# Sparse attention and a Sinkhorn mixture of experts on one core: four edits of order

## The chip, the core and the metric

The kernel runs on one core of a Trainium2 chip. A core has five engines with queues of their own: TensorE (PE in the profile, with its weight loads as PEld), VectorE (DVE), ScalarE (ACT), GpSimd (POOL) and SyncE (SP). They run side by side and wait for each other through semaphores. Matmuls write into PSUM banks; all other tiles lie in SBUF. The metric is the time of one execution on the device, in microseconds (us).

## What is computed

First eight heads of attention over four batches of 576 tokens. Four heads see the 32 tokens up to and with their own; the other four see every 32nd token up to their own. The result, 2304 tokens of 512 values, is x. Then a gate over eight experts, made even over tokens and experts in eight rounds, and the experts.

```python
scores = np.where(masks[None, :, :, :], scale * q @ k.T, -1000000000.0)
attn = np.exp(scores - np.max(scores, axis=-1, keepdims=True))
attn = attn / (np.sum(attn, axis=-1, keepdims=True) + 1e-09)
x = (attn @ v).transpose(0, 2, 1, 3).reshape(2304, 512)

logits = x @ w_gate
P = np.exp(logits - logits.max())
for _ in range(8):
    P /= P.sum(1, keepdims=True) + 1e-09
    P /= P.sum(0, keepdims=True) + 1e-09
    P *= N / E
for e in range(8):
    out += P[:, e:e + 1] * (np.maximum(x @ w1[e], 0.0) @ w2[e])
```

## The kernel before, in words

**Two parts for precision.** Every operand of a large matmul is held as a high part (ScalarE copies it to the matmul's own type) and a low part (source minus high part, made by VectorE or POOL). A product is then three matmuls: high by high, high by low, low by high.

**The start and the slots.** Attention runs in 32 units (batch, pair of heads, half), one after the other. For each: a load of queries and keys (qk) and one of values (v) by load_qkv, the scores on PE, the mask and the smallest value on VectorE (L247, which reads the constants cst), the exponential on ScalarE (L259), the normalization on POOL (L270), transposes on PE (L282, against the identity in cst), the product with the values (L295, L309), and x in two parts (L331 on ScalarE, L336 on VectorE). The first eight units stand in a loop of their own (at_k to WARM). Behind it come 36 slots. A slot takes 256 tokens and one of four column blocks of the first half of expert 0: its first layer (L417), the second layer of the slot before (L454), and, while there are units left, a unit's values, the next unit's scores, and then the transposes and the normalization of units between. The table `work` adds further pieces to the end of a slot.

**Units of x sums.** The rest of the experts runs with Strassen's scheme: 768 tokens at a time (a pass; there are three) and 256 columns (a pair of 128), seven products instead of eight. The sums of x that it needs are made by build_s for 128 tokens at a time, as one of the pieces in `work`: in one slot two L532 and four L548 on POOL, in the next slot a high part on ScalarE (L551) and a low part on VectorE (L553), and in the one after that two stores (L556). Units for passes 0 and 1 stand in slots named in a list.

**Steps.** After the slots, step(g) runs for each group g, 30 groups in each pass. A step finishes the first layer of the group before (finish_first), begins its own seven products (ba, bb and bc are their banks; L698) and does the second layer of the group before. In pass 0 the second layer is an ordinary one (second, L730), and the step also prepares the weights of the next group: load_w1g brings the raw W1 (ra, rb), prep_w1 makes three sums on POOL (L616, L619, L620) and splits all four (L177 on ScalarE, L178 on POOL); load_w2g brings the raw W2, whose sums (L649 to L653) and low parts VectorE makes. In passes 1 and 2 the prepared weights come back from memory, and the second layer is Strassen's too (second_strassen, L849): its seven left sides are a11, a22, a12 and the four sums s1 to s4, each with a high part (L830, ScalarE) and a low part (L834, POOL). In finish_first the sums themselves are made on POOL (L906 to L910) out of the gated results u3, m1, r11 and u2. Their order on POOL is the order of the program. The first group of a pass copies its second products with ScalarE (total, L855) in place of adding them with VectorE (L857).

**The gate's rounds.** The generator `gat` gives one round of the eight at each next(gat): a small product (L382) between VectorE's reductions and divisions (L374 to L386). The last rounds run in step 0.

**Queues.** SP issues all loads and stores in the order of the program, except the first constants, which ScalarE's queue issues (L1061). A DMA that must wait holds up those behind it on its queue. The sets of PSUM banks are named t, l1, s and y, two banks each.

Of the kernel before, what the change touches and what calls it, by code (L numbers as in the profile page):

```python
# [55 lines left out]
def kernel(  # L56
# [9 lines left out]
    nc = tc.nc  # L66
    P = 128
    NT, D = out.shape
    E, _, F = w1.shape
# [32 lines left out]
    cst = const.tile([P, 4, P], F32, name="cst")  # L102
# [54 lines left out]
    def load_w2(t, e, f0):  # L157
        nc.sync.dma_start(t, w2[e, f0 : f0 + P, :])
# [37 lines left out]
    qkv_t, sms, sums_t, pts, moved, mxs = {}, {}, {}, {}, {}, {}  # L196

    def load_qkv(k):
        if k < NS:
            nq, nk, nv = _columns(*steps[k][1:])  # L200
            t = pools["qkv"].tile([P, QK], F32, tag="qk", name=f"qk_{k}", bufs=3)
            nc.sync.dma_start(t[:, : nq + nk], qkv[k, :, : nq + nk])
            tv = pools["qkv"].tile([P, 5 * 2 * DH], F32, tag="v", name=f"v_{k}", bufs=5)
            nc.sync.dma_start(tv[:, :nv], qkv[k, :, nq + nk : nq + nk + nv])
            qkv_t[k] = t, tv[:, :nv].rearrange("p (w j d) -> p w j d", j=2, d=DH)
# [270 lines left out]
    at = W1N  # L476
# [29 lines left out]
    for p in range(NPASS):  # L506
        for k in range(NK):
            k = (k - KEEP * p) % NK
# [61 lines left out]
    def load_w1g(g):  # L570
        if g >= NK or g in wraw:
            return
        _, e, j, _ = groups[g]
        if g < 2:
            t = raw_slots(4).rearrange("p (n i k f) -> p n i k f", n=4, i=2, k=2)
            wraw[g] = [t[:, i] for i in range(4)]
        else:
            wraw[g] = [
                pools["hg" if g == 2 else "rab"].tile(
                    [P, 2, 2, P], F32, tag=f"r{x}", name=f"r{x}_{g}",  # L580
                    bufs=2 if g > 2 and x in "ab" else 1,
                )
                for x in "abtu"
            ]
        ra, rb = wraw[g][:2]
        for t, i, dh, fh in ((ra, 0, 0, 0), (ra, 1, 1, 1), (rb, 0, 0, 1), (rb, 1, 1, 0)):
            f0 = f_at(g, fh)
            nc.sync.dma_start(
                t[:, i],
                w1[e, 2 * P * dh : 2 * P * (dh + 1), f0 : f0 + P].rearrange("(k p) f -> p k f", p=P),  # L590
            )

    def load_w2g(g):
        if g >= NK:
            return
        _, e, j, _ = groups[g]
        o = 2 * D * ((g + 1) % 2)
        w2raw[g] = raws[:, o : o + 2 * D]
        for i in range(2):
            load_w2(w2raw[g][:, i * D : (i + 1) * D], e, f_at(g, i))  # L600
# [109 lines left out]
    def turning(g):  # L710

        return g >= NK and g % NK == NK - LAST[groups[g][0]]
# [119 lines left out]
    def form_lo(g, name, src):  # L832
        t = hg[g, name]
        nc.gpsimd.tensor_tensor(t[:, 1], src, t[:, 0].bitcast(F32), op=ALU.subtract)  # L834
# [49 lines left out]
    def finish_first(g, s):  # L884

        m1, u2, u3, bb, bc = part.pop(g)
        mul(g, "t4", "x22", bb, False)
        if s:
            gated(g, u3, u3, 1)
            form_hi(g, "a22", u3)  # L890
        plus(m1, bb, m1)
        if s:
            gated(g, m1, m1, 1)
        else:
            relu_hi(g, 1, 0, m1)
        mul(g, "w22", "s4", bc, False)
        plus(u2, bc, u2)
        if not s:
            relu_hi(g, 0, 1, u2)
            return ((1, 0, m1), (0, 1, u2))  # L900
        gated(g, u2, u2, 0)
        r11 = r11s.pop(g)
        s1, s4 = (
            pools["late"].tile([P, TN], F32, tag=x, name=f"{x}_{g}") for x in ("s1t", "s4t")
        )
        nc.gpsimd.tensor_tensor(s1, m1, u3, op=ALU.add)  # L906
        nc.gpsimd.tensor_tensor(m1, m1, r11, op=ALU.subtract)
        nc.gpsimd.tensor_tensor(r11, s1, r11, op=ALU.subtract)
        form_lo(g, "a22", u3)
        nc.gpsimd.tensor_tensor(s4, u2, r11, op=ALU.subtract)  # L910
        return ("a12", u2), ("s2", r11), ("s3", m1), ("s1", s1), ("s4", s4)

    def step(g):
# [2 lines left out]
        s = strassen(G)  # L916
        w1n, w2n = prep_w1(g + 1), prep_w2(g)
        if new:
            load_w1g(g + 2)
            if G in spans:  # L920
                load_gate(spans.index(G) + 1)
        late = ()
# [2 lines left out]
        if g >= NK:  # L925
            next(w1n, None)
        load_w2g(g + 1)
        if turning(G):
            combine()
        if new:  # L930
            m1, u2, u3 = (
                pools["u"].tile([P, TN], F32, tag=x, name=f"{x}_{g}", bufs=2)
                for x in ("m1", "u2", "u3")
            )
# [123 lines left out]
        load_qkv(at_k + 2)  # L1058

    WARM = 2 * NP - 1  # L1060
    nc.scalar.dma_start(cst[:, :2], consts[:, :2])  # L1061
    load_qkv(0)
    load_qkv(1)
    load_w()
    load_qkv(2)
    load_w()
# [61 lines left out]
    def at(i, f, *x):  # L1128
        work.setdefault(i, []).append(lambda: f(*x))

    gat = gating()
    units = [(p, k, P * th) for p in range(2) for k in range(2) for th in range(3)]
    for x, i in zip(units, (8, 9, 10, 11, 12, 13, 18, 19, 20, 21, 22, 23)):
        w = build_s(*x, P, True)
        for n in range(3):
            at(i + n, next, w, None)
# [7 lines left out]
    ):  # L1144
        at(i, load_x, 0, name)
    at(29, lambda: later_store.pop()())
    at(34, load_w1g, 2)
    at(28, load_w2g, 0)
    for i in (27, 27, 28, 28, *range(29, 35)):
        work.setdefault(i, []).insert(0, lambda: next(gat))  # L1150
# [76 lines left out]
    for g in range(NG + 1):  # L1227
# [20 lines left out]
        if 0 < p < NPASS:  # L1248
            i = n - 3
# [85 lines left out]
```

## Time and profile before

| | |
|---|---|
| three runs shown | 1550.41, 3234.23, 3856.46 us (median 3234.23) |
| the profiled execution | 1549.56 us |
| its span, first to last instruction | 1547.4 us, 25973 instructions |
| mean granted clock of TensorE | 1.00 of full speed |
| PE busy | 1535.4 us (99%) |
| weight loads (PEld) busy | 1456.0 us (94%) |
| VectorE busy | 1312.3 us (85%) |
| POOL busy | 1054.9 us (68%) |
| ScalarE busy | 548.1 us (35%) |
| moved by DMA | 430.49 MB, mean 278 GB/s |
| chain that ended last | PE 97%; POOL, DVE, DMA and issue 1% each |

How to read it: every share is of the span. The chain is the work that ended last, followed back from the last instruction; at each step it goes to what released it. Matmuls are pipelined, and their ends are modelled, so a wait of PE can also show as a group of matmuls that takes longer than the same group elsewhere. An idle time in front of an instruction stands in brackets, with what ended it.

### The profile page before, as it was taken

The page shows a single profiled execution, that of the slowest core. Times are in us where ns is not written, and L with a number is a line of the kernel's source. Part 1 is how long each engine was busy: PE and PEld are TensorE (multiplying, and loading weights), DVE is VectorE, ACT ScalarE, POOL GpSimd, SP SyncE. Part 2 cuts the span into 40 slices and gives each one's busy share as a digit, 9 for nine tenths or more (in the row PEclk, how much of TensorE's full clock was granted, in tenths as well). Part 3 has the DMA queues.
Part 4 walks back from the last instruction along what each step waited for, and adds up shares of the span by engine and source line. Part 5 has one row for each costly group of instructions (what it writes and reads, how often), then busy time and mean ns, then how long its engine had stood idle before and what let it go on. Part 6 is the DMA issues. An engine that isn't in the chain of part 4 may idle for free.

```text
span 1547.4 us, 25973 instructions
## 1 busy us (share of the span) xinstructions
PE 1535.4 (99%) x9188; PEld 1456.0 (94%) x9188; DVE 1312.3 (85%) x2552; ACT 548.1 (35%) x1299; POOL 1054.9 (68%) x1069
## 2 busy tenths in 40 slices
PE   7999999999999999999999999999999999999999
PEld 6888889898989898999999999999999999999998
DVE  5676699999999999868888888888688888888888
ACT  6666244343434343333232223223322332222221
POOL 4387255555656556168888888887777777877874
PEclk9999999999999999999999999999999999999999
DMA  7577977988989898887877777776676766766662
GB/s 226 179 235 237 377 285 289 350 324 314 327 318 328 318 328 324 299 318 274 305 282 289 267 279 286 266 283 255 245 277 262 294 256 243 284 245 246 280 241 93
DMA packets 144704, 430.49 MB, mean 278 GB/s; under 512 B 34912, under 2 KB 89280, under 8 KB 129600
## 3 DMA queue, kind: packets, MB, share of 16 engines
q1 hardware_dynamic: 144432, 428.71, 74.4%
q8 instruction: 73, 1.20, 0.3%
q14 instruction: 55, 0.45, 0.1%
q10 hardware_dynamic: 144, 0.13, 0.0%
HBM read 284.05 MB, written 144.75 MB: 277 GB/s over the span
## 4 chain that ended last, share of the span: by engine, by line
PE 97%; POOL 1%; DVE 1%; DMA 1%; issue 1%; ACT 0%; SPq 0%; POOLq 0%; DVEq 0%
PE p L849 27%; PE bb L698 18%; PE yg L730 17%; PE bc L698 12%; PE ba L698 12%; PE y L454 3%; PE ph L417 3%; PE tp L282 1%; DMA qk<-in_qkv 1%; PE sc L234 1%; PE pv L295 1%; PE pl L345 1%; PE pv L309 1%; PE sc L220 1%; POOL sm L270 0%
## 5 line engine op out<-in xcount | busy, mean ns | idle before, releaser
L857 DVE TENSOR_TENSOR total<-p,total 128x384 f32<-128x384 f32 x770 | 400.7, 557 | 0.8 <-PE p L849 0.8
L698 PE MATMUL bb<-reg 128*128 128x384 f32 x1620 | 325.8, 335 | 0.0
L698 PEld LDWEIGHTS bb<-reg 128*128 128x128 f32 x1620 | 285.0, 188 | 2.8 <-DVE u L772 0.3
L698 PE MATMUL bc<-reg 128*128 128x384 f32 x1080 | 216.4, 334 | 0.0
L698 PE MATMUL ba<-reg 128*128 128x384 f32 x1080 | 216.2, 334 | 0.0
L830 ACT ACTIVATE a<-u 128x384 fp32r<-128x384 f32 x114 | 59.9, 526 | 384.1 <-DVE u L824 382.6
L772 DVE TENSOR_TENSOR u<-bb,m 128x384 f32<-128x384 f32 x180 | 99.9, 555 | 112.9 <-PE bb L698 110.2
L698 PEld LDWEIGHTS bc<-reg 128*128 128x128 f32 x1080 | 190.0, 188 | 0.0
L698 PEld LDWEIGHTS ba<-reg 128*128 128x128 f32 x1080 | 189.8, 188 | 0.0
L906 POOL TENSOR_TENSOR s1t<-m,u 128x384 f32<-128x384 f32 x57 | 57.9, 1016 | 162.8 <-DVE m L824 162.8
L737 DVE SCALAR_TENSOR_TENSOR acc<-yg,gate,acc 128x512 f32<-128x512 f32 x197 | 139.0, 740 | 9.0 <-PE yg L730 9.0
L730 PE MATMUL yg<-w2t,h 128*128 128x512 f32 x540 | 125.5, 390 | 0.0
L730 PE MATMUL yg<-w2b,h 128*128 128x512 f32 x540 | 125.4, 390 | 0.0
L849 PE MATMUL p<-s,w2b 128*128 128x384 f32 x696 | 125.3, 334 | 0.0
L849 PEld LDWEIGHTS p<-s,w2b 128*128 128x128 f32 x696 | 121.1, 188 | 0.0
L849 PE MATMUL p<-s,w2t 128*128 128x384 f32 x672 | 121.0, 334 | 0.0
L730 PEld LDWEIGHTS yg<-w2b,h 128*128 128x128 f32 x540 | 101.1, 188 | 20.5
L730 PEld LDWEIGHTS yg<-w2t,h 128*128 128x128 f32 x540 | 101.1, 188 | 20.5
L834 POOL TENSOR_TENSOR a<-u,a 128x384 fp32r<-128x384 f32 x114 | 117.0, 1027 | 0.0
L849 PEld LDWEIGHTS p<-s,w2t 128*128 128x128 f32 x672 | 116.9, 188 | 0.0
L178 POOL TENSOR_TENSOR reg<-ra,reg 128x512 fp32r<-128x512 f32 x28 | 47.1, 1681 | 89.0 <-ACT reg L177 89.0
L772 DVE TENSOR_TENSOR u<-bc,u 128x384 f32<-128x384 f32 x180 | 99.5, 553 | 4.7 <-PE bc L698 1.4
(152 smaller groups left out, 2853.7 us busy)
## 6 DMA issues: line engine op xcount, KB each, us to landing
reg<-wd SPq DMA_DIRECT2D x56, 1792.0 KB
wd<-reg SPq DMA_DIRECT2D x30, 1792.0 KB
w2b<-w2d SPq DMA_DIRECT2D x27, 1792.0 KB
w2t<-w2d SPq DMA_DIRECT2D x26, 1792.0 KB
w2d<-w2b SPq DMA_DIRECT2D x15, 2048.0 KB
w2d<-w2t SPq DMA_DIRECT2D x15, 2048.0 KB
raws<-in_w SPq DMA_DIRECT2D x68, 256.0 KB
reg<-sd SPq DMA_DIRECT2D x12, 768.0 KB
```

The costliest lines, as they stand in the source:

```text
L178: nc.gpsimd.tensor_tensor(lo, src, hi.bitcast(F32), op=ALU.subtract)
L417: nc.tensor.matmul(ph[:, :n], w[:, i, dt, :], xv(x, dt, c0, n), start=(first and len(taken) == 1 and i + x == 0), stop=(len(taken) == NDT ...
L454: nc.tensor.matmul(y, h[:, a, i * P : (i + 1) * P], w[:, b, :], start=(ft == 0 and first), stop=(ft == FH - 1 and a == 1),)
L698: nc.tensor.matmul(out[:, :TN], w[:, i, k, :], xops[x][:, xi, k, :], start=(start and n == 0), stop=(n == 5), skip_group_check=True,)
L730: nc.tensor.matmul(y, hg[g, i // 3, f][:, a, o : o + P], w[:, b, f, :], start=(f == 0 and a + b == 0), stop=(f == 1 and a == 1),)
L737: nc.vector.scalar_tensor_tensor(acc[:, i, :], y, gate[:, t, e : e + 1], acc[:, i, :], op0=ALU.mult, op1=ALU.add)
L772: nc.vector.tensor_tensor(o, bank[:, :TN], s, op=ALU.add)
L830: nc.scalar.activation(t[:, 0], src, AF.Copy)
L834: nc.gpsimd.tensor_tensor(t[:, 1], src, t[:, 0].bitcast(F32), op=ALU.subtract)
L849: nc.tensor.matmul(y[:, :TN], w[:, b, wi, d, :], h[:, a, :], start=(a + b == 0), stop=(a == 1),)
L857: nc.vector.tensor_tensor(o, y[:, :TN], o, op=ALU.add)
L906: nc.gpsimd.tensor_tensor(s1, m1, u3, op=ALU.add)
```

## The change

Four edits. The first constants go from ScalarE's queue to SP's, behind the queries and keys of the first unit; the values of the first two units follow behind the queries and keys of the second. In the list of slots for build_s, 8, 9, 10 become 7, 8, 9: the slot 10 is taken out and a slot 7 put in. The load of the raw W1 of group 2 goes from the end of slot 34 into step 0, behind load_w2g. In finish_first the low part of a22 stands ahead of the four sums instead of ahead of the last.

```diff
--- before.py
+++ after.py
@@ -196,10 +196,15 @@
     qkv_t, sms, sums_t, pts, moved, mxs = {}, {}, {}, {}, {}, {}
 
     def load_qkv(k):
+        for _ in load_qkv_parts(k):
+            pass
+
+    def load_qkv_parts(k):
         if k < NS:
             nq, nk, nv = _columns(*steps[k][1:])
             t = pools["qkv"].tile([P, QK], F32, tag="qk", name=f"qk_{k}", bufs=3)
             nc.sync.dma_start(t[:, : nq + nk], qkv[k, :, : nq + nk])
+            yield
             tv = pools["qkv"].tile([P, 5 * 2 * DH], F32, tag="v", name=f"v_{k}", bufs=5)
             nc.sync.dma_start(tv[:, :nv], qkv[k, :, nq + nk : nq + nk + nv])
             qkv_t[k] = t, tv[:, :nv].rearrange("p (w j d) -> p w j d", j=2, d=DH)
@@ -903,10 +908,10 @@
         s1, s4 = (
             pools["late"].tile([P, TN], F32, tag=x, name=f"{x}_{g}") for x in ("s1t", "s4t")
         )
+        form_lo(g, "a22", u3)
         nc.gpsimd.tensor_tensor(s1, m1, u3, op=ALU.add)
         nc.gpsimd.tensor_tensor(m1, m1, r11, op=ALU.subtract)
         nc.gpsimd.tensor_tensor(r11, s1, r11, op=ALU.subtract)
-        form_lo(g, "a22", u3)
         nc.gpsimd.tensor_tensor(s4, u2, r11, op=ALU.subtract)
         return ("a12", u2), ("s2", r11), ("s3", m1), ("s1", s1), ("s4", s4)
 
@@ -916,7 +921,8 @@
         s = strassen(G)
         w1n, w2n = prep_w1(g + 1), prep_w2(g)
         if new:
-            load_w1g(g + 2)
+            if g:
+                load_w1g(g + 2)
             if G in spans:
                 load_gate(spans.index(G) + 1)
         late = ()
@@ -925,6 +931,8 @@
         if g >= NK:
             next(w1n, None)
         load_w2g(g + 1)
+        if not g:
+            load_w1g(2)
         if turning(G):
             combine()
         if new:
@@ -1058,9 +1066,12 @@
         load_qkv(at_k + 2)
 
     WARM = 2 * NP - 1
-    nc.scalar.dma_start(cst[:, :2], consts[:, :2])
-    load_qkv(0)
-    load_qkv(1)
+    first = [load_qkv_parts(k) for k in range(2)]
+    next(first[0])
+    nc.sync.dma_start(cst[:, :2], consts[:, :2])
+    next(first[1])
+    for x in first:
+        next(x, None)
     load_w()
     load_qkv(2)
     load_w()
@@ -1130,7 +1141,7 @@
 
     gat = gating()
     units = [(p, k, P * th) for p in range(2) for k in range(2) for th in range(3)]
-    for x, i in zip(units, (8, 9, 10, 11, 12, 13, 18, 19, 20, 21, 22, 23)):
+    for x, i in zip(units, (7, 8, 9, 11, 12, 13, 18, 19, 20, 21, 22, 23)):
         w = build_s(*x, P, True)
         for n in range(3):
             at(i + n, next, w, None)
@@ -1144,7 +1155,6 @@
     ):
         at(i, load_x, 0, name)
     at(29, lambda: later_store.pop()())
-    at(34, load_w1g, 2)
     at(28, load_w2g, 0)
     for i in (27, 27, 28, 28, *range(29, 35)):
         work.setdefault(i, []).insert(0, lambda: next(gat))
```

On SP, the first rows of the program (the number behind a name's first number is a buffer's). Before:

```order
L202 DMA qk_0_115<-in_qkv 128x504
L204 DMA v_0_117<-in_qkv 128x256
L202 DMA qk_1_119<-in_qkv 128x648
L204 DMA v_1_121<-in_qkv 128x384
L171 DMA raws_105<-in_w1 128x4x128
```

After:

```order
L206 DMA qk_0_114<-in_qkv 128x504
L1071 DMA cst_97<-in_consts 128x256
L206 DMA qk_1_117<-in_qkv 128x648
L209 DMA v_0_119<-in_qkv 128x256
L209 DMA v_1_121<-in_qkv 128x384
L171 DMA raws_105<-in_w1 128x4x128
```

The constants now stand second on SP, v_0 has moved from second to fourth, and all from v_1 on stands one place further back.

On POOL, the end of slots 7 to 10 (sm is the normalization of a unit, sx a unit of x sums). Before:

```order
L270 TENSOR_TENSOR sm_14_0_1000<-sm_14_0_1000,sums_14_999 128x480
L270 TENSOR_TENSOR sm_15_0_1082<-sm_15_0_1082,sums_15_1081 128x480
L532 TENSOR_TENSOR sx_0_0_0_1187<-reg_107 128x2x128 x2
L548 TENSOR_TENSOR sx_0_0_0_1187<-sx_0_0_0_1187 128x128 x4
L270 TENSOR_TENSOR sm_16_0_1148<-sm_16_0_1148,sums_16_1147 126x252
L270 TENSOR_TENSOR sm_16_1_1152<-sm_16_1_1152,sums_16_1147 126x252
L532 TENSOR_TENSOR sx_0_0_128_1279<-reg_107 128x2x128 x2
L548 TENSOR_TENSOR sx_0_0_128_1279<-sx_0_0_128_1279 128x128 x4
L270 TENSOR_TENSOR sm_17_0_1238<-sm_17_0_1238,sums_17_1237 108x324
L270 TENSOR_TENSOR sm_17_1_1243<-sm_17_1_1243,sums_17_1237 108x324
L532 TENSOR_TENSOR sx_0_0_256_1365<-reg_107 128x2x128 x2
```

After:

```order
L275 TENSOR_TENSOR sm_14_0_1000<-sm_14_0_1000,sums_14_999 128x480
L537 TENSOR_TENSOR sx_0_0_0_1116<-reg_107 128x2x128 x2
L553 TENSOR_TENSOR sx_0_0_0_1116<-sx_0_0_0_1116 128x128 x4
L275 TENSOR_TENSOR sm_15_0_1082<-sm_15_0_1082,sums_15_1081 128x480
L537 TENSOR_TENSOR sx_0_0_128_1197<-reg_107 128x2x128 x2
L553 TENSOR_TENSOR sx_0_0_128_1197<-sx_0_0_128_1197 128x128 x4
L275 TENSOR_TENSOR sm_16_0_1155<-sm_16_0_1155,sums_16_1154 126x252
L275 TENSOR_TENSOR sm_16_1_1159<-sm_16_1_1159,sums_16_1154 126x252
L537 TENSOR_TENSOR sx_0_0_256_1291<-reg_107 128x2x128 x2
L553 TENSOR_TENSOR sx_0_0_256_1291<-sx_0_0_256_1291 128x128 x4
L275 TENSOR_TENSOR sm_17_0_1248<-sm_17_0_1248,sums_17_1247 108x324
L275 TENSOR_TENSOR sm_17_1_1253<-sm_17_1_1253,sums_17_1247 108x324
```

Each of the first three units stands one slot earlier, and behind the normalization of unit 17, at the end of slot 10, no x sums follow.

On SP, from the end of slot 35 into step 1 (ra and rb are the raw W1 of a group, raws here the raw W2, sd the x sums). Before:

```order
L588 DMA ra_2_2970<-in_w1 128x2x128 x2
L588 DMA rb_2_2971<-in_w1 128x2x128 x2
L564 DMA reg_107<-sd_109 128x1536
L158 DMA raws_105<-in_w2 128x512 x2
L1205 DMA yd_111<-acc_104 128x512 x2
```

After:

```order
L569 DMA reg_107<-sd_109 128x1536
L158 DMA raws_105<-in_w2 128x512 x2
L593 DMA ra_2_3002<-in_w1 128x2x128 x2
L593 DMA rb_2_3003<-in_w1 128x2x128 x2
L1215 DMA yd_111<-acc_104 128x512 x2
```

The four loads for group 2 have gone behind the last x sums and the raw W2. In finish_first the order on POOL is a22's low part, s1, m1, r11, s4 where it was s1, m1, r11, a22's low part, s4, in each of 57 steps.

## Rows read from the trace of the kernel before

**Rows 1.** Busy time by stretch: start:end, length, busy (instructions), PEclk, DMA share, GB/s.

```profile
0.00:40.00 40.00, 32.12 (x340) 25.03 (x341) 24.12 (x150) 27.37 (x122) 19.24 (x27) 1.00 0.70 225
40.00:200.00 160.00, 159.26 (x1467) 137.18 (x1466) 108.45 (x467) 85.52 (x330) 87.21 (x125) 1.00 0.77 255
...
0.00:1547.40 1547.40, 1535.37 (x9188) 1456.00 (x9188) 1312.29 (x2552) 548.14 (x1299) 1054.92 (x1069) 1.00 0.75 278
```

**Rows 2.** Timeline: start, length, engine, line, operation [idle before, releaser]; the start.

```profile
0.73 0.40 ACTq L1061 DMA_DIRECT2D cst<-in_consts  x1
...
1.19 0.44 SPq L204 DMA_DIRECT2D v<-in_qkv  x1
...
5.35 0.29 DVE L247 CUSTOM_DVE_ANT_0 sm<-sc,cst 126x126 f32<-126x126 f32 x1 [5.35 <-PE sc L234]
```

**Rows 3.** The chain that ended last, in order of time: start, length, what.

```profile
0.74 3.33 DMA qk<-in_qkv
...
30.73 2.88 DMA qk<-in_qkv
```

**Rows 4.** Timeline of slots 10 and 11: VectorE's L553, POOL's L532, PE's transposes.

```profile
83.50 1.92 DVE L553 TENSOR_TENSOR so<-sx,so 128x512 fp32r<-128x512 f32 x1 [0.98 <-ACT so L551]
...
84.14 1.87 POOL L532 TENSOR_TENSOR sx<-reg 128x256 f32<-128x256 f32 x2
...
86.29 0.46 PE L282 MATMUL tp<-cst,sm 108*108 108x108 f32 x3 [0.25 <-DVE reg L336]
```

**Rows 5.** The tile so (duration min/median/max in ns), and VectorE's timeline after slot 8.

```profile
L553 DVE TENSOR_TENSOR so<-sx,so x12: 691/942/1917, 78.0 to 155.6; 128x512 fp32r<-128x512 f32 x12
...
73.50 0.42 DVE L435 SCALAR_TENSOR_TENSOR h<-ph,h 128x256 fp32r<-128x256 f32 x1 [0.52 <-ACT h L434]
74.30 0.55 DVE L336 TENSOR_TENSOR reg<-pv,reg 128x192 fp32r<-128x192 f32 x2 [0.38 <-ACT reg L331]
```

**Rows 6.** Timeline of the last gate rounds: VectorE, POOL and PE.

```profile
190.91 0.31 DVE L377 TENSOR_TENSOR gate<-gate,g 128x144 f32<-128x144 f32 x1
...
195.06 0.98 DVE L377 TENSOR_TENSOR gate<-gate,g 128x144 f32<-128x144 f32 x1
...
194.58 1.30 POOL L616 TENSOR_TENSOR rt<-rb,ra 128x512 f32<-128x512 f32 x1 [30.09 <-DVE g L374]
...
196.54 0.39 PE L382 MATMUL pc<-g,ones 128*128 128x8 f32 x2 [0.33 <-DVE g L379]
```

**Rows 7.** Busy time by stretch: two microseconds of step 0 (columns as in rows 1).

```profile
198.00:200.00 2.00, 2.00 (x11) 1.68 (x10) 1.90 (x7) 0.68 (x2) 0.37 (x1) 1.00 0.00 0
```

**Rows 8.** Timeline of VectorE and PE in steps 1 and 2.

```profile
201.08 0.42 DVE L652 TENSOR_TENSOR w2sum<-raws,w2sum 128x256 f32<-128x256 f32 x1
...
202.35 0.55 DVE L772 TENSOR_TENSOR u<-bc,u 128x384 f32<-128x384 f32 x1
...
213.65 1.46 DVE L652 TENSOR_TENSOR w2sum<-raws,w2sum 128x256 f32<-128x256 f32 x1
...
203.82 1.20 PE L698 MATMUL bc<-reg 128*128 128x384 f32 x6
```

**Rows 9.** Timeline of pass 2's first Strassen group, and a steady step's 18 matmuls.

```profile
1109.12 1.02 POOL L906 TENSOR_TENSOR s1t<-m,u 128x384 f32<-128x384 f32 x1 [8.51 <-DVE m L824]
...
1113.45 1.04 POOL L910 TENSOR_TENSOR s4t<-u,r 128x384 f32<-128x384 f32 x1
1113.57 3.63 PE L849 MATMUL p<-a,w2b 128*128 128x384 f32 x18
...
1115.37 4.96 ACT L855 ACTIVATE total<-p 128x384 f32<-128x384 f32 x11
...
890.91 3.28 PE L849 MATMUL p<-a,w2t 128*128 128x384 f32 x18
```

**Rows 10.** PE's timeline: the same 16 matmuls of scores at two times.

```profile
17.92 0.92 PE L220 MATMUL sc<-qk 64*64 64x96 f32 x16
...
20.94 0.56 PE L220 MATMUL sc<-qk 64*64 64x96 f32 x16
```

## The prediction

> **What bounds the kernel now.** I read busy time by stretch, then the chain of work that ended last, and last the timeline at each place that the change touches. The reader is to see one thing first: TensorE (PE) is busy for 1535.37 of 1547.40 us, so all the other engines together leave it idle for 12.0 us. Of these, 7.9 us lie in the first 40 us, 0.7 between 40 and 200, and 3.4 in all the rest [rows 1]. The change removes no matmul. It can only gain what PE loses by waiting at the places that it touches, and it costs what it makes PE wait anew. 2% of this kernel is 31 us, about what a measurement of it can tell from no change, and more than twice all of PE's idle time.
>
> The sum is made against the profiled execution: 1549.56 us, of which the span is 1547.4, with 2.2 us around it. The three runs shown are 1550.41, 3234.23 and 3856.46, median 3234.23. The profiled execution stands 0.85 below the lowest, and at less than half of the median. Its granted clock is 1.00, the upper of the two levels (2.4 GHz), over the whole span [rows 1]. With PE that busy, no waiting that this program holds doubles the time; my forecast is for an execution like the profiled one.
>
> **The change, part by part.** There are four edits, each at a place of its own.
>
> *The constants go from ScalarE's queue to the second place on SP's.* Now ACT issues them at 0.73 us [rows 2], beside the first queries and keys, which SP issues at 0.74 and which land 3.33 us later on the chain; the first matmul starts with that landing [rows 3]. The same kind of load later on the chain takes 2.88 [rows 3]. If the constants beside it are what makes 3.33 of 2.88, the first matmul starts sooner. Bounds: nothing (the difference is something else) and 3.33 - 2.88 = 0.45. I take 0.25, about the middle, and count it in full, since the chain of the first 40 us starts from this landing and passes through work. What is put later: the constants leave at 1.19, which is v_0's place now [rows 2]; with the 3.33 of their neighbour they land at 4.52. VectorE reads them first at 5.35 [rows 2], 5.1 with the gain: covered by 0.6, and one for one were they later than that. v_0 moves two places back and every load behind one place, 0.45 a place (from 0.74 to 1.19); the first matmuls that read v come after the scores, the softmax and the transposes. Cost taken: nothing. The Trainium skill (DMA: Bandwidth & Descriptors, section Issuing engines are not separate DMA queues) speaks against this edit: loads issued from several engines share the same 16 DMA engines and interleave, and a second issuing engine saves just the issue time. If that issue time is all there is, the edit gives up a free issue of 0.4 us and this term is 0, the sum 0.68 instead of 0.93. The trace has only this one pair of loads that start together, so it cannot tell.
>
> *The first three units' x sums run in slots 7, 8 and 9; slot 10 has none.* Each unit is two L532 and four L548 on POOL in its slot, and one L553 on VectorE in the next. Slot 10 now has an L553 of 1.92 us at 83.50, with POOL's L532 pair at 84.14 inside it [rows 4]; the fastest L553 takes 0.69 [rows 5]. The x parts behind it on VectorE are late, and the second transposes of slot 11 wait 0.25 us for them [rows 4]. After, slot 10 still has an L553 (the third unit's), but no L532 beside it. Bounds: a gain of 0.25, and a loss of 0.25, the same stall once more, since slot 8 now has an L553 too, ahead of the h part at 73.50. Behind that place VectorE has idle time of 0.52 and 0.38 us [rows 5]; an L553 of 1.92 would push the x parts at 74.30 (0.55 long) by 1.0, to 75.9. If it is 0.69, all of it falls into the idle time. I take a gain of 0.15: nearer the gain, since the L532 pair leaves slot 10, but something may be handed on from slot 8.
>
> *The third pair's raw W1 is loaded in step 0, behind w2.* Its four issues go from ahead of the last slots' work to behind raws. What this moves is POOL: the three sums of the third pair run as soon as the load lands, now at 194.58, in the last sinkhorn rounds [rows 6]. There VectorE's L377 takes 0.98 us where the round before took 0.31, and PE then waits 0.33 for the L379 behind it [rows 6]. After, I put these sums at about 198: the DMA engines moved nothing from 198 to 200 [rows 7], so all was landed by then, and the same bytes are asked for. L377 then stands alone, its round ends 0.67 sooner, and the wait of 0.33 is gone. What is late next: the sums run beside the w2 sums on VectorE; one of these takes 0.42 at 201.08 and, in the next step beside POOL, 1.46 at 213.65 [rows 8]. Behind them VectorE reads the bank that PE overwrites at 203.82; it is done with it at 202.35 + 0.55 = 202.90 [rows 8], a cover of 0.92. One such operation hit (1.04 later) makes PE wait 0.1, one and a half 0.6. Bounds: a gain of 0.33, and a loss of 0.6 - 0.33 = 0.27. I take the gain: POOL should be through its longest sum before VectorE begins.
>
> *The low part of a22 goes ahead of the four sums.* In every Strassen step POOL waits for m at s1t; where pass 2 begins, that wait is 8.51 us long [rows 9], and the moved part (1.04 us, as s4t there) fits into it as soon as its high part is there. In the steady steps PE has no wait that this could remove: 18 matmuls take 3.28 us [rows 9]. Where pass 2 begins, the 18 take 3.63 [rows 9]. There s4t starts at 1113.45 on POOL, ScalarE's part of it follows, and behind that on ScalarE the first copy of total at 1115.37, which frees the bank that the 13th matmul writes [rows 9]. PE wants it at 1113.57 + 12 x 0.173 = 1115.65, and the copy (4.96 / 11 = 0.45) ends at 1115.82. After, s4t starts up to 1.04 sooner (less, where the moved part itself pushes s1t). Bounds: nothing, and 3.63 - 3.28 = 0.35. I take 0.20: the wait that the copy explains is 0.17 and goes with the first quarter of a microsecond.
>
> The sum: 0.25 + 0.15 + 0.33 + 0.20 = 0.93 us less, 1549.56 - 0.93 = 1548.6 us. All bounds together run from 1549.56 - 0.45 - 0.25 - 0.33 - 0.35 = 1548.2 to 1549.56 + 0.25 + 0.27 = 1550.1.
>
> **The rivals.** *A wait takes the place of the one removed:* the L553 in slots 8 to 10, or the w2 sums in step 1. For it: one VectorE operation that meets POOL costs 0.7 to 1.2 [rows 5, 6], and the cover in step 1 is 0.92. Against it: in both places the moved work goes to where POOL had been idle. Without the two terms (0.48) the time is 1549.1; at their loss bounds, 1549.56 - 0.45 + 0.52 = 1549.6. Chance 0.20.
>
> *A transfer that is hidden anyway, and a change that does nothing:* the 3.33 us are the first load's own time, and PE's 18 matmuls wait for something other than s4t. Against the first stands the 2.88. 1549.56 - 0.48 = 1549.1. Chance 0.10.
>
> *PE gets fast later (the other side).* 16 matmuls take 0.92 us at 17.92 and the same 16 take 0.56 at 20.94 [rows 10]. The granted clock reads 1.00 on the span as a whole [rows 1], so that column does not show it, yet the rows get faster between 18 and 21 us. If that point comes later, each microsecond costs up to 0.39 of itself (1 - 0.56 / 0.92) where PE is full. The gain of 0.93 is eaten from 2.4 us on; 5 us later, 1548.6 + 1.95 = 1550.6. If it comes sooner by as much, 1548.6 - 1.95 = 1546.7; ahead of 18 us PE is not full, which makes this end less likely. The Trainium skill (TensorE: Matmul & The Clock Gate, section What's actually happening) says that the moment at which the clock is released isn't tied to the kernel's start and so differs between runs. By that rule an earlier first matmul may move the point either way; one trace can't show it. Chance 0.13 for later, 0.07 for sooner.
>
> **How the numbers follow.** Forecast 0.50 (1548.2 to 1549.0), a wait in its place 0.20 (1549.1 to 1549.6), nothing at the two ends 0.10 (1549.1), PE fast later 0.13 (1549.6 to 1550.6), sooner 0.07 (1546.7 to 1548). Two executions of the one kernel already differ by 0.85. A range of 1546.9 to 1550.8 holds all but the far ends of the clock cases and some of this spread, about 0.15 left out. No case comes near 31 us: a wait of 0.5 us in every one of some 60 steps would be needed, and the steady steps keep their loads. I leave 0.03 for faster by over 2% and 0.03 for slower, for what no row shows; within 2% has 0.94.
>
> **What would show it.** Right: the first load on the chain at about 3.1 us instead of 3.33; no wait at the second transposes of slot 11; L377 of the last round at 0.31 us and no PE wait for L379; POOL's three sums at about 198; the 18 matmuls at the start of pass 2 at about 3.4 us; PE idle for 11.1 us in all. Wrong: 3.3 on the chain still; VectorE waiting for the constants; L553 at 1.9 in slot 8 or 9 with a PE wait behind it; a PE wait at bc in step 1; the slow matmuls ending at another time than 18 to 21 us.

## The result, and the profile after

The changed kernel takes 1563.49 us (median of six runs, 1562.88 to 1564.16). The kernel before takes 1549.20 to 1550.41 in the four runs beside them; two more, the long ones among the three shown ahead of the prediction, are left out here and below. The ratio is 1.0088, with a 95% interval of 1.0073 to 1.0103: 0.88% slower. That is less than the 2% named in the prediction, so the case "within 2%" is what happened, but its interval lies clear of 1, its sign is the wrong one, and the time lies 12.7 us above the top of the range (1550.8). The profiled execution took 1562.88 us with a span of 1561.0, against 1549.56 and 1547.4: 13.6 us more span.

The line numbers are a few higher after: VectorE's gating (L824 before) is L829, its addition of two banks (L772) L777, the products of the steps (L698) L703, the second layer's products (L849) L854, the low parts (L834) L839, the first sum s1t (L906) L912. The page of the changed kernel, busy time by engine:

```profile
PE 1549.0 (99%) x9188; PEld 1453.9 (93%) x9188; DVE 1350.9 (87%) x2552; ACT 542.1 (35%) x1299; POOL 1058.2 (68%) x1069
```

Two things are to be seen against [rows 1]. VectorE does the same 2552 instructions in 1350.9 us instead of 1312.3: 38.6 us more. And TensorE's idle time is 1561.0 - 1549.0 = 12.0 us, the same as before, although the kernel is 13.6 us longer: the same 9188 matmuls are busy for 13.6 us more. Waits that are spread thin over a stream of matmuls don't show as idle PE, since the modelled end of one matmul lies behind the start of the next. They show in front of the weight loads. The groups of the changed kernel, ordered by cost (busy, mean ns of one, idle just before them, what ended it):

```profile
L703 PE MATMUL bb<-reg 128*128 128x384 f32 x1620 | 331.9, 339 | 0.8
L703 PEld LDWEIGHTS bb<-reg 128*128 128x128 f32 x1620 | 282.6, 188 | 19.7 <-DVE u L777 17.2
```

and its waits (who waits for whom: us in all, how many, the longest):

```profile
POOL a L839 <- ACT a L835: 164.4, 58, 25.5
POOL s1t L912 <- DVE m L829: 29.9, 55, 0.6
PEld bb L703 <- DVE u L777: 17.2, 53, 0.3
```

The same views of the kernel before read:

```profile
POOL s1t L906 <- DVE m L824: 162.8, 57, 8.5
POOL a L834 <- ACT a L830: 25.9, 1, 25.9
PEld bb L698 <- DVE u L772: 0.3, 1, 0.3
```

So a wait of PE for VectorE's addition, which came once before, comes 53 times. POOL's wait moved as intended, from the first sum (s1t, which waits for m) to the low part of a22 (which waits for its high part). What happens to VectorE is seen when its groups are kept apart by shape. The gating of m (VectorE's product of m with the gate), after and before:

```profile
L829 DVE SCALAR_TENSOR_TENSOR m<-m,raws 128x384 f32<-128x384 f32 x57 | 75.9, 1332 | 2.0
```

```profile
L824 DVE SCALAR_TENSOR_TENSOR m<-m,raws 128x384 f32<-128x384 f32 x57 | 31.8, 558 | 2.0
```

One operation, same size, same number, 1332 ns instead of 558: 44 us. The timeline of one ordinary step tells why, and what it costs. After:

```profile
872.79 0.56 DVE L777 TENSOR_TENSOR m<-bb,m 128x384 f32<-128x384 f32 x1
873.34 1.01 POOL L839 TENSOR_TENSOR a<-u,a 128x384 fp32r<-128x384 f32 x1 [2.26 <-ACT a L835]
873.38 1.38 DVE L829 SCALAR_TENSOR_TENSOR m<-m,raws 128x384 f32<-128x384 f32 x1
...
874.90 1.02 POOL L912 TENSOR_TENSOR s1t<-m,u 128x384 f32<-128x384 f32 x1 [0.56 <-DVE m L829]
875.26 1.08 DVE L829 SCALAR_TENSOR_TENSOR u<-u,raws 128x384 f32<-128x384 f32 x1
...
876.27 0.55 DVE L777 TENSOR_TENSOR u<-bb,m 128x384 f32<-128x384 f32 x1
...
876.86 1.01 PEld L703 LDWEIGHTS bb<-reg 128*128 128x128 f32 x6 [0.34 <-DVE u L777]
876.87 1.32 PE L703 MATMUL bb<-reg 128*128 128x384 f32 x6
```

and the same step before:

```profile
870.96 0.56 DVE L824 SCALAR_TENSOR_TENSOR m<-m,raws 128x384 f32<-128x384 f32 x1
871.66 1.02 POOL L906 TENSOR_TENSOR s1t<-m,u 128x384 f32<-128x384 f32 x1 [2.72 <-DVE m L824]
872.02 1.07 DVE L824 SCALAR_TENSOR_TENSOR u<-u,raws 128x384 f32<-128x384 f32 x1
...
873.49 0.56 DVE L772 TENSOR_TENSOR u<-bb,m 128x384 f32<-128x384 f32 x1 [0.40 <-PE bb L698]
...
874.10 1.05 PEld L698 LDWEIGHTS bb<-reg 128*128 128x128 f32 x6
```

The high part of a22 is ready just as VectorE begins to gate m. POOL starts the low part at 873.34, VectorE the gating at 873.38, and the gating takes 1.38 us: it ends 0.41 behind POOL's operation. VectorE then has 0.82 us less for its chain: the gating of u, and the addition that empties bank bb, into which PE's next product goes. Before, that addition waited 0.40 for PE and ended 0.05 ahead of the next weight load; there was no more slack than that. After, it starts 2.89 behind the start of the gating instead of 2.53, and PE waits 0.34. From one s1t to the next, the steps last 14.84 us on average instead of 14.57 in pass 1, and 14.87 instead of 14.58 in pass 2. 53 times 0.27 to 0.29 make 14.3 to 15.4 us; the span is only 13.6 longer, since the changed kernel is ahead elsewhere. The chain of the changed kernel in order of time, and before, at the last second layer ahead of the first Strassen step:

```profile
656.07 8.20 PE yg L735 x36
```

```profile
656.94 8.20 PE yg L730 x36
```

Up to here the change had gained 0.87 us. All of the loss comes behind this point.

### The profile page after: what moved, and what is told of

It is laid out like the page before. It is cut to its first block, busy times and chain, and to the rows that moved or that the text cites. A ratio compares the mean times of both kernels' runs of the same rounds, so it can differ in the third digit from the quotient of the medians.

```text
span 1561.0 us, 25968 instructions
## 1 busy us (share of the span) xinstructions
PE 1549.0 (99%) x9188; PEld 1453.9 (93%) x9188; DVE 1350.9 (87%) x2552; ACT 542.1 (35%) x1299; POOL 1058.2 (68%) x1069
## 4 chain that ended last, share of the span: by engine, by line
PE 98%; POOL 1%; ACT 0%; issue 0%; DMA 0%; DVE 0%; POOLq 0%; DVEq 0%
PE p L854 26%; PE bb L703 19%; PE yg L735 17%; PE bc L703 12%; PE ba L703 12%; PE y L459 3%; PE ph L422 3%; PE tp L287 1%; PE sc L239 1%; PE pv L300 1%; PE pv L314 1%; PE pl L350 1%; PE sc L225 1%; DMA qk<-in_qkv 0%; POOL sm L275 0%
## 5 line engine op out<-in xcount | busy, mean ns | idle before, releaser
L703 PE MATMUL bb<-reg 128*128 128x384 f32 x1620 | 331.9, 339 | 0.8
L703 PEld LDWEIGHTS bb<-reg 128*128 128x128 f32 x1620 | 282.6, 188 | 19.7 <-DVE u L777 17.2
L703 PE MATMUL bc<-reg 128*128 128x384 f32 x1080 | 216.7, 335 | 0.0
L703 PE MATMUL ba<-reg 128*128 128x384 f32 x1080 | 216.3, 334 | 0.0
L839 POOL TENSOR_TENSOR a<-u,a 128x384 fp32r<-128x384 f32 x114 | 116.8, 1025 | 138.9 <-ACT a L835 138.9
L703 PEld LDWEIGHTS bc<-reg 128*128 128x128 f32 x1080 | 189.9, 188 | 0.5 <-DVE u L777 0.3
L703 PEld LDWEIGHTS ba<-reg 128*128 128x128 f32 x1080 | 189.8, 188 | 0.4 <-ACT m L949 0.4
L777 DVE TENSOR_TENSOR u<-bb,m 128x384 f32<-128x384 f32 x180 | 99.2, 551 | 89.1 <-PE bb L703 87.0
L854 PE MATMUL p<-s,w2b 128*128 128x384 f32 x696 | 125.3, 334 | 0.0
L854 PEld LDWEIGHTS p<-s,w2b 128*128 128x128 f32 x696 | 121.1, 188 | 0.0
L854 PE MATMUL p<-s,w2t 128*128 128x384 f32 x672 | 121.0, 334 | 0.0
L854 PEld LDWEIGHTS p<-s,w2t 128*128 128x128 f32 x672 | 116.9, 188 | 0.0
L777 DVE TENSOR_TENSOR u<-bc,u 128x384 f32<-128x384 f32 x180 | 99.2, 551 | 4.4 <-PE bc L703 1.3
L854 PE MATMUL p<-a,w2b 128*128 128x384 f32 x522 | 95.6, 335 | 0.2 <-ACT total L860 0.2
```

The source lines that it names most:

```text
L703: nc.tensor.matmul(out[:, :TN], w[:, i, k, :], xops[x][:, xi, k, :], start=(start and n == 0), stop=(n == 5), skip_group_check=True,)
L777: nc.vector.tensor_tensor(o, bank[:, :TN], s, op=ALU.add)
L854: nc.tensor.matmul(y[:, :TN], w[:, b, wi, d, :], h[:, a, :], start=(a + b == 0), stop=(a == 1),)
```

## The experiments

Each comparison is with runs of the kernel before on the same chip, 27 to 34 of them, whose medians were 1549.63 to 1549.85.

**The changed kernel without its fourth edit, and the fourth edit alone.** In the first, the low part goes back to its place before; in the second, it is all that is changed.

```diff
 # changed kernel -> e1
-        form_lo(g, "a22", u3)
         nc.gpsimd.tensor_tensor(s1, m1, u3, op=ALU.add)
         nc.gpsimd.tensor_tensor(m1, m1, r11, op=ALU.subtract)
         nc.gpsimd.tensor_tensor(r11, s1, r11, op=ALU.subtract)
+        form_lo(g, "a22", u3)
```

> The changed kernel with only the order of a22's low part put back behind r11. Theory 1 (VectorE's gating of m and POOL's low part of a22 meet in SBUF: 0.56 to 1.38 us, of which some 0.27 a step reach PE, in 57 steps): the Strassen steps go back to 14.57 us, L829 on m to 0.56, and the time is about 0.9 us under the kernel before. Theory 2 (the four sums start later on POOL, and their parts come late to the second layer): the same time, since this undoes the order too; the two are told apart in other runs. Theory 3 (the three other edits shift the whole and the Strassen steps run in another phase to their loads): the steps stay at 14.84 us, some 13 us over the kernel before.

Measured: 1548.99 us, ratio 0.9996 (0.9987 to 1.0004).

> The kernel before with a22's low part put first and nothing else. Theories 1 and 2: 57 steps longer by 0.27 us less what the starts of the passes gain, about +14.5 us. Theory 3: about the time of before.

Measured: 1563.92 us, ratio 1.0091 (1.0077 to 1.0104); +14.2 us. Its waits, and then its groups by shape:

```profile
PEld bb L698 <- DVE u L772: 17.1, 53, 0.3
```

```profile
L824 DVE SCALAR_TENSOR_TENSOR m<-m,raws 128x384 f32<-128x384 f32 x57 | 75.5, 1325 | 2.0
```

The fourth edit makes the whole loss, and with it come the long gating and the 53 waits; without it both are gone (558 ns, one wait). No other edit is needed for it.

**The low part behind all four sums.** If the trouble were the order of POOL's work as such, a place still later for the low part should cost something too, or move the loss.

```diff
 # changed kernel -> e4
-        form_lo(g, "a22", u3)
         ...
         nc.gpsimd.tensor_tensor(s4, u2, r11, op=ALU.subtract)
+        form_lo(g, "a22", u3)
```

> The changed kernel with a22's low part behind all four sums. Theory 1: nothing of POOL's lies on VectorE's gating of m but what lay there before, so the steps take 14.57 us; s4 comes 1.0 us sooner, which takes the 0.35 us at the start of pass 2 away: 0.2 to 0.4 us under the version with the order put back, 1.1 to 1.3 under the kernel before. Theory 2 (what counts is how late the parts of the left sides come): a22's own low part is 1.0 us later and is the second wanted, so PE waits in each step, up to 0.5 us, +20 us or more.

Measured: 1548.78 us, ratio 0.9992 (0.9983 to 1.0001); the gating is at 558 ns and the steps at 14.57 us. PE does not need the low part early. Where pass 2 begins, the 18 matmuls of [rows 9] take less, in this kernel and then in the one without the fourth edit:

```profile
1113.41 3.33 PE L854 MATMUL p<-a,w2b 128*128 128x384 f32 x18
```

```profile
1113.71 3.59 PE L854 MATMUL p<-a,w2b 128*128 128x384 f32 x18
```

That is 0.26 for the place that the fourth edit aimed at: s4t goes ahead of the low part here as well, and nothing is laid beside the gating of m.

**One input of the gating out of SBUF.** The changed kernel, with the low part first; VectorE's gating of m reads its second input from a PSUM bank; the gate itself is left out of m.

```diff
 # changed kernel -> e6
-            gated(g, m1, m1, 1)
+            nc.vector.scalar_tensor_tensor(
+                m1, m1, 0.0, bb[:, :TN], op0=ALU.max, op1=ALU.mult)
```

> The changed kernel, a22's low part first, with the gate of VectorE's operation on m (L829, the one that grew to 1.38 us) read from the PSUM bank bb in place of the gate tile in SBUF, so that one of its two inputs lies in SBUF; m is multiplied by the wrong values. Theory 1a (two inputs from SBUF beside a POOL operation that reads SBUF): L829 on m is back at 0.56 us and the steps at 14.57, about 1548.8 us, though POOL does all that it did. Theories 1b and 2: no change, 1563 us.

Measured: 1548.51 us, ratio 0.9992 (0.9982 to 1.0001). A step's timeline, and then the group by shape:

```profile
885.18 1.02 POOL L839 TENSOR_TENSOR a<-u,a 128x384 fp32r<-128x384 f32 x1 [1.05 <-ACT a L835]
885.23 0.55 DVE L899 SCALAR_TENSOR_TENSOR m<-m,bb 128x384 f32<-128x384 f32 x1
```

```profile
L899 DVE SCALAR_TENSOR_TENSOR m<-m,bb 128x384 f32<-128x384 f32 x57 | 31.6, 554 | 2.0
```

The two operations lie over each other as in the changed kernel (0.05 apart), and the gating takes 0.55. The loss is gone, though POOL's order is that of the changed kernel. So it is not the order, and not the mere fact that the two engines work at the same time: this operation of VectorE is held up when both its inputs lie in SBUF, and not with one of them in PSUM. (The last section shows another operation that is held up with a single input in SBUF.)

**Zero fills on POOL.** Two runs ask the same from POOL's side, with an operation that only writes. In the first, three fills stand in place of the low part.

```diff
 # changed kernel -> e5
-        form_lo(g, "a22", u3)
+        for _ in range(3):
+            nc.gpsimd.memset(hg[g, "a22"][:, 1].bitcast(F32), 0.0)
```

> The changed kernel with a22's low part replaced, in the same place ahead of the four sums, by three fills of that tile with zeros on POOL; the low part of a22 is left out of the result. POOL is still busy beside VectorE's gating of m, but reads nothing. Theory 1a (the two meet where both read SBUF): L829 on m takes 0.56 us and the steps 14.57, about 1548.8 us. Theory 1b (they meet where both write, or POOL being busy there is enough): L829 stays near 1.38 us and the steps near 14.84, about 1563 us. Theory 2 (a late s1 on POOL): if the fills take as long as the low part, s1 is late as before and the steps are 14.84.

Measured: 1547.88 us, ratio 0.9987 (0.9978 to 0.9996), the gating at 558 ns. But the fills wait for nothing that the low part had waited for, and ran early (867.21 to 868.59, the gating of that step at 870.16). They did not overlap, so this run tells nothing about the meeting; it only shows again that a step without it costs nothing. The second keeps the wait: two fills of u3, which must follow ScalarE's copy of it, are added to the kernel before.

```diff
 # kernel before -> e12
+        for _ in range(2):
+            nc.gpsimd.memset(u3, 0.0)
         nc.gpsimd.tensor_tensor(s1, m1, u3, op=ALU.add)
```

> The kernel before, with two fills of u3 with zeros on POOL at the place of a22's low part ahead of the four sums; the low part stays behind r11. A fill must wait until ScalarE has read u3, so it falls on VectorE's gating of m in every step, as the low part did; u3 is left out of s1 and of a22's low part. Theory 1a (the POOL operation must read SBUF): L824 on m stays at 0.56 us, the steps at 14.57, the time within 1 us of the kernel before. Theory 1b (any POOL operation on SBUF blocks it): L824 on m at 1.0 us or more, the steps at up to 14.84, up to +14 us.

Measured: 1551.99 us, ratio 1.0012 (1.0003 to 1.0022); +2.1 us. A step's timeline, and then the group by shape:

```profile
871.19 0.90 POOL L907 MEMSET u<- 128x384 f32 x2 [1.55 <-ACT a L830]
871.25 0.56 DVE L824 SCALAR_TENSOR_TENSOR m<-m,raws 128x384 f32<-128x384 f32 x1
```

```profile
L824 DVE SCALAR_TENSOR_TENSOR m<-m,raws 128x384 f32<-128x384 f32 x57 | 31.8, 557 | 2.0
```

Now they do overlap: the gating lies wholly inside the 0.90 us of the two fills, and in all 57 steps it stays at 557 ns; ordinary steps take 14.57. These fills, which only write, do not hold VectorE up. The time is above the 1 us expected: POOL has more to do in all, and where the passes begin PE waits for ScalarE's first copy of total, 0.67 us at 1117.12 (0.37 at 674.55). The profiled span is 1.4 longer, of which these two waits are 1.0; no run tests them.

**The other three edits, alone and together.**

The constants go behind the first queries with the values of both units behind the second (e7); the x sums move (e8); the load goes into step 0, behind load_w2g (e9). e3 has the edits of e7 and e8.

```diff
 e7 -    nc.scalar.dma_start(cst[:, :2], consts[:, :2])
 e7 +    nc.sync.dma_start(cst[:, :2], consts[:, :2])
 e8 -    ... (8, 9, 10, 11, 12, 13, ...)
 e8 +    ... (7, 8, 9, 11, 12, 13, ...)
 e9 -    at(34, load_w1g, 2)
 e9 +        if not g:
 e9 +            load_w1g(2)
```

> The kernel before with the constants' edit alone. From the changed kernel's trace: the first matmul at 3.5 us instead of 4.1, the second unit's scores wait for their load at 5.8, and 0.36 us of the 0.62 are left at 40 us: 0.3 to 0.4 us under the kernel before. With the x sums' edit beside it the whole was 1.3 under, so the x sums are then worth about 0.9; if this run gives 0.6, they are worth 0.7.

Measured: 1549.39 us, ratio 0.9998 (0.9989 to 1.0007): -0.24 against 1549.63.

> The kernel before with the x sums' edit alone. If the edits add up (both together 1.34 under, the constants alone 0.24 under): 1.1 us under the kernel before. The changed kernel's trace shows 0.43 in slot 11 and 0.20 in slot 12, thus 0.6; the rest would then be spread between executions.

Measured: 1548.54 us, ratio 0.9994 (0.9985 to 1.0002): -1.3 against 1549.85.

> The kernel before with the load's edit alone. The pair with and without it showed 1548.99 against 1548.34, so it costs 0.65 there. If what it costs is VectorE's w2 sums beside POOL's three sums whatever stands ahead: 0.3 to 0.7 over the kernel before. If it costs only because PE comes 1.0 us sooner there, and not where PE does not: 0.3 under, as predicted.

Measured: 1550.19 us, ratio 1.0003 (0.9994 to 1.0011): +0.3 against 1549.85.

> The constants' edit and the x sums' edit alone. If the load's edit gives nothing on balance (PE's 0.62 at the last gate rounds is given back in steps 1 and 2, where VectorE's w2 sums meet POOL): 1.0 us under the kernel before, as much as or 0.1 more than without a22's edit alone. If the load's edit keeps its 0.33: 0.5 to 0.6 under the kernel before.

Measured: 1548.34 us, ratio 0.9992 (0.9983 to 1.0001): -1.3 against 1549.68, and 0.65 below the kernel that has the load edit too (1548.99). All these intervals hold 1 or touch it. By their medians the x sums gain, the load loses, and the constants do next to nothing, but none of the three can be told from no change by these runs. What each edit does is read from traces, in the next section.

**Towards a better kernel.** The edits of the constants and of the x sums, with the low part last; and then the same with the mask alone behind the first queries and the identity behind the second.

```diff
 # e3 -> e10: form_lo(g, "a22", u3) behind the sum s4
 # e10 -> e13
-    nc.sync.dma_start(cst[:, :2], consts[:, :2])
+    nc.sync.dma_start(cst[:, 1:2], consts[:, 1:2])
     next(first[1])
+    nc.sync.dma_start(cst[:, 0:1], consts[:, 0:1])
```

> The constants' and the x sums' edits, the load where it was before, and a22's low part behind all four sums. If the gains add up: 1.34 us for the two edits and some 0.2 to 0.3 for a22's place, 1.5 to 1.7 under the kernel before. If the gain at the start of pass 2 is given back behind it: 1.3 under.

Measured: 1548.38 us, ratio 0.9991 (0.9983 to 1.0000): 1.25 under the kernel before, so the gains did not add up to 1.5.

> The version with the constants' and x sums' edits and a22 last (1548.38), with only the first mask second on SP, and the identity behind the second unit's queries and keys. The second unit's scores wait for their load in the changed kernel (1.12 us, at 5.83). If the 64 KB less ahead of it count: the second load lands 0.2 to 0.3 us sooner and as much is left at 40 us, 1548.1. If the load's time is set by other things: no difference.

Measured: 1548.62 us, ratio 0.9995 (0.9986 to 1.0004). The second unit's scores do start 0.18 sooner (5.67 for 5.85), but the first logits come 0.56 later (59.34 for 58.78), in one trace of each. Neither kernel is below the x sums alone (1548.54) by more than the runs of one kernel differ. What is left to gain here is about 1.3 us, 0.08%, and cannot be told from nothing with certainty.

## Why the prediction was wrong

**The step that failed is the fourth edit's cost.** The prediction took the gap ahead of s1t on POOL as free time: "the moved part fits into it", and in the steady steps "PE has no wait that this could remove". Both are true of POOL and of PE in an ordinary step (POOL waited 2.72 there, 871.66 above). The bounds were "nothing, and 0.35": no side with a loss. What was not looked at is the engine between the two. POOL waited for m, that is, for VectorE's gating of m; filling this wait with POOL's work puts that work onto exactly this VectorE operation, in every step. The bracket in [rows 9] said so ("<-DVE m L824"). The price was in the trace too: the gating of u, the same operation and size, takes 1.07 beside s1t (872.02 above) and 0.55 where POOL doesn't lie over it, and the prediction itself used such prices (0.98 for 0.31 in [rows 6], 1.46 for 0.42 in [rows 8]) for two other edits. And VectorE's slack in an ordinary step, 0.40 at the addition that follows, was one row away. With the prices that the trace held, 1.07 - 0.55 = 0.52 to 1.46 - 0.42 = 1.04, each of the 57 steps would have had a wait of 0.12 to 0.64: a loss of 7 to 36 us, at either end far above the range. It came to 0.82 on VectorE, and to about 0.3 on PE. The sentence "a wait of 0.5 us in every one of some 60 steps would be needed, and the steady steps keep their loads" had the right form and the wrong premise.

The gain of 0.20 where pass 2 begins did not come either. Timeline of the changed kernel there (before: [rows 9]):

```profile
1114.77 0.56 DVE L829 SCALAR_TENSOR_TENSOR m<-m,raws 128x384 f32<-128x384 f32 x1
1114.91 1.30 POOL L839 TENSOR_TENSOR a<-u,a 128x384 fp32r<-128x384 f32 x1 [8.08 <-ACT a L835]
1116.17 1.32 POOL L912 TENSOR_TENSOR s1t<-m,u 128x384 f32<-128x384 f32 x1
...
1119.77 1.03 POOL L915 TENSOR_TENSOR s4t<-u,r 128x384 f32<-128x384 f32 x1
1119.86 2.24 PE L854 MATMUL p<-a,w2b 128*128 128x384 f32 x12
...
1122.33 1.33 PE L854 MATMUL p<-a,w2b 128*128 128x384 f32 x6 [0.23 <-ACT total L860]
```

The gap is 8.08 us long, but the moved part has to wait for its high part and starts only when m is being gated too, so it pushes s1t: s1t starts 3.69 ahead of the 18 matmuls instead of 4.45. That takes back what s4t was to win (0.09 ahead of them now, 0.12 before), and the 18 take 3.80 for 3.63. The prediction had set "up to 1.04 sooner (less, where the moved part itself pushes s1t)" and counted 0.20 all the same. The cause that it named was right: the version with the low part last has s4t sooner, and the 18 take 3.33.

The Trainium skill (SBUF — State Buffer, section Who interferes with whom) has the rule for it: a VectorE instruction with two SBUF inputs contends with a GpSimd instruction that reads SBUF, not with one that only writes, and whichever was issued first blocks the other. The trace agrees on each count: 1.38 us where POOL started 0.04 ahead and reads; 0.55 with one input in a PSUM bank; 0.56 beside the fills; and where the gating itself started 0.14 ahead (1114.77 above), it took 0.56 and POOL's operation 1.30. The prediction did not weigh this rule; with it, and with the slack of 0.40, the fourth edit would have had a loss in each step.

**The rival of a new wait** was named, for L553 and for the w2 sums, at the two places where the edit moved more than one operation, and not for this one. **PE fast later** was given 0.13 as the rival on the slow side, and set the top of the range. The point at which the matmuls get fast did move between the kernels (16 matmuls of scores take 0.59 at 17.44 in the kernel without the fourth edit, 0.92 still at 17.59 in the changed kernel with the low part last), and yet the first logits come at 58.65 and 58.78 there, against 59.11 before. It explains nothing of the loss: PE is 0.87 ahead at 656. **"PE idle for 11.1 us in all"** was named as a sign of a right prediction; the idle time stayed at 12.0 while the time grew by 13.6, so this view could not have shown it.

**The constants (0.25 predicted).** The first load lands sooner by more than assumed, and the second one eats most of it. Chain and timeline of the changed kernel:

```profile
0.74 2.71 DMA qk<-in_qkv
...
5.83 1.42 PE L239 MATMUL sc<-qk 64*108 64x108 f32 x12 [1.12 <-DMA qk<-in_qkv]
```

2.71 for 3.33 [rows 3] is 0.62, more than the bound of 0.45; the second unit's scores then wait 1.12 for their queries, which are issued at 1.66 as before (1.68). They start at 5.83 where they started at 5.92: 0.09 is left of 0.62 there, and 0.36 at 59 us (the first logits at 58.75 for 59.11). The term's size was about right, by luck, for its working was not: it asked whether the constants and v_0 come late, and not what the next load, which comes no sooner, then limits. In the profiled execution of the edit alone the second load lands later still (scores at 6.42), and the first logits come at 59.32, 0.21 later than before. Over all traces the first matmul starts at 3.44 to 3.56 in the nine kernels with the edit and at 4.04 to 4.11 in the five without; the first logits come at 58.48 to 58.78 in seven of the nine, at 59.32 and 59.34 in the two others, and at 59.05 to 59.12 without it. So the landing is shown, and what is left of it is not a fixed amount. The Trainium skill (DMA: Bandwidth & Descriptors, section Issuing engines are not separate DMA queues) says that loads issued by several engines interleave on the same DMA engines: the trace agrees (0.62 sooner without the second one). The prediction drew from its other sentence that the term would be 0; that is not so for the landing, while for the whole kernel the runs of the edit alone (0.24, an interval that holds 1) can't tell.

**The x sums (0.15 predicted).** No L537 (L532 before) stands in slot 10, and the second transposes of slot 11 wait for nothing. Timeline of the changed kernel, the first layers of slots 12 and 13 (86.52 and 91.38 before):

```profile
85.73 1.67 PE L422 MATMUL ph<-reg,w 128*128 128x256 f32 x12
90.39 1.67 PE L422 MATMUL ph<-reg,w 128*128 128x256 f32 x12
```

0.79 and 0.99 ahead, of which 0.36 come from the start: 0.43 in slot 11 and 0.20 in slot 12, whose four transposes take 0.59 instead of 0.80; and no wait is handed on from slots 7 to 9. The mechanism was right and the term four times too small: the one bracket of 0.25 was not all that slot 10's meeting cost. The edit alone measured 1.3; what the further 0.7 is stays open. Part of it may be luck: its trace has no wait of PE for L379 in the last gate rounds (0.33 in [rows 6]), where POOL's sums happened to start later, at 194.91 for 194.58.

**The load (0.33 predicted).** The first half came: L382 (L377 before) takes 0.31 and PE no longer waits there. The second did not. "POOL should be through its longest sum before VectorE begins" is the step that failed: it came true, and was not enough. Timeline of the changed kernel:

```profile
196.93 1.30 POOL L621 TENSOR_TENSOR rt<-rb,ra 128x512 f32<-128x512 f32 x1 [33.44 <-DVE u L777]
...
198.31 1.15 POOL L624 TENSOR_TENSOR ru<-ra,rt 128x256 f32<-128x256 f32 x1
198.79 1.22 DVE L654 TENSOR_TENSOR w2sum<-raws 128x512 f32<-128x512 f32 x1
...
200.04 0.84 DVE L657 TENSOR_TENSOR w2sum<-raws,w2sum 128x256 f32<-128x256 f32 x1
...
202.33 1.01 PEld L703 LDWEIGHTS bc<-reg 128*128 128x128 f32 x6 [0.28 <-DVE u L777]
...
203.69 1.01 PEld L703 LDWEIGHTS ba<-reg 128*128 128x128 f32 x6 [0.35 <-ACT m L949]
```

The first sum is over before the w2 sums begin; the second and third meet the w2 sums, 1.22 for 0.69 and 0.84 for 0.42, 0.95 more together, and PE waits at bc and ba in step 1, 0.63 in all, as the rival had it (0.6). Without the fourth edit bc waits 0.66 there. It is the same meeting of engines as above, once per kernel instead of 57 times.

## What to carry to other kernels

An engine's wait is not free room for its work: look up what the engine that it waits for is doing then, and whether the two may run side by side, before a step is moved into the gap. In a loop of many equal steps, the first number to read is the slack of each engine next to the bound one in an ordinary step (here 0.4 us on VectorE), for a loss just above it comes back at every step. And where one engine is busy for 99%, the idle time that a profile gives it is no bound: not on what can be lost, and not on what can be won either, for the changed kernel is idle for the same 12.0 us, and undoing its fourth edit wins 14.5 (1548.99 for 1563.49). The prediction began with this bound.

## What was new about the hardware

- A VectorE operation with both inputs in SBUF (128x384, f32) took 1.38 us for 0.56 when a POOL operation of 1.01 that reads SBUF had started 0.04 before it; with one input in PSUM it took 0.55, beside POOL's zero fills 0.56. It ended 0.41 behind POOL's operation. Where it started 0.14 ahead of POOL's operation, it took 0.56 and POOL's 1.30 for 1.01.
- It isn't the size of the operation that counts, and two inputs in SBUF are not always needed: in the last gate rounds of the kernel with the constants' edit alone, an operation with one input of 128x18 values takes as long as POOL's sum beside it, 1.30 where it takes 0.17 in the changed kernel. Its timeline:

```profile
194.71 1.30 POOL L621 TENSOR_TENSOR rt<-rb,ra 128x512 f32<-128x512 f32 x1 [30.05 <-DVE g L379]
194.73 1.30 DVE L380 TENSOR_SCALAR g<-g 128x18 f32<-128x18 f32 x1
...
197.47 0.39 PE L387 MATMUL pc<-g,ones 128*128 128x8 f32 x2 [1.08 <-DVE g L384]
```

PE waits 1.08 there, for 0.33 in [rows 6]. Not every operation with one input is held up: in the kernel with the edits of the constants and the x sums, VectorE's reciprocal of 18 values (L381, at 193.50) took its usual 0.27 inside POOL's sum (193.35 to 194.64). Which operation is hit depends on when POOL's first sum starts: at 193.35 to 195.41 in the eight kernels that leave its load where it was, and at 194.58 and 195.41 in the kernel before and the one with the fourth edit alone, whose programs are the same up to there. So a difference of half a microsecond between two traces may be no more than this.
- The first load landed 0.62 sooner (2.71 us for 3.33) once the constants' load, which ScalarE's queue had issued 0.01 before it, was gone.
